# A gated mix of two attentions: gate, table and beta moved into the projections, a third buffer of q, and one output piece per run at the end

## Chip, cores and metric

The kernel runs on one core of a Trainium2 chip. The metric is the device time of one execution in microseconds (us). Before the change it is 1905.45 us, the median of three runs (1904.41 to 1909.33).

## What is computed

The reference, cut to what matters (S = 2048, D = 512, 32 heads of 16):

```
g = sigmoid((x * gate_w).sum(-1))            # one gate per row
a = softmax(q k' / 4) v @ A_wo               # side A: full attention, all rows
b = side B: per segment of 512 rows, causal softmax attention, mixed with a memory:
      o = sigmoid(beta) * a_mem + (1 - sigmoid(beta)) * a_dot      # one beta per head
      a_mem = phi(q) M / (phi(q) z);  then M += phi(k)' v, z += sum phi(k)
      b = o @ B_wo
out = g * a + (1 - g) * b
```

phi(t) is t + 1 for t > 0 and exp(t) otherwise.

## The kernel before

**Two stages.** The first, the projections, makes q, k and v of both sides and the memory's parts, and leaves them in DRAM tiles. The second, the attention, reads them back. The order of the instructions is written out by hand, for each engine, with no scheduler.

**The projections run in slots.** A slot (`slot`) is the 12 matmuls of one projection tile of 128 x 512: four steps of the contraction, three products each, since every operand is split into a rounded part and a rest. After each third matmul there is a place where posted work is issued: `post(slots, place, f)` counts from now, `post_at(n, place, f)` names the slot. Slots 0 to 47 are side A (for each of four chunks of 512 rows: four tiles of q, four of k, four of v), 48 to 95 are side B (q, v, k). `qk_tile` is a q or k tile: in the slot behind its matmuls ScalarE copies the PSUM tile out (`full`, L370) and casts it (`q1`, L371), VectorE takes the rest (`q2`, L378), and SP's queue stores both to DRAM (L372, L379). PSUM has two such tiles (`pr`), so a tile must be copied out before the second slot after its own begins. `q1` and `q2` have two buffers each. On side B, a tile with `then` also gets phi: a minimum on GpSimd (L375, tile `mn`), an exponential on ScalarE (L382), a sum on VectorE.

**Gate and beta.** `load_gate` (L456) brings 512 rows of x and, four and five slots later, `gate_logit` makes their logits on VectorE (L453). When all slots are through, the logits are transposed on TensorE, ScalarE makes the sigmoid (L572), VectorE one minus it, and GpSimd's queue stores both (L575); the attention's first exponential (L661) follows on ScalarE. Beta is brought spread over the partitions by eight loads on GpSimd's queue (L446, L449), and its sigmoids are made when side A's projections are through (L478, L479). ScalarE has its functions in tables, and the profile shows a load (ACT_TABLE_LOAD) where it goes from sigmoid to exponential or back.

**The attention runs in slots too.** There are 2368, 64 for each of 32 units of A (four heads, one chunk of queries) and 10 for each of 32 units of B. A slot makes one score tile (`st`, L638, three PSUM banks) and its exponential (L661). Side by side with it, 96 slots ahead (`LEAD`), runs a product for the row maxima (`sm`, L204, four banks) with its reduction on VectorE (L219). After each third slot (`BURST`) comes a run of P @ V (`some_values`, L694), and then at most one or two pieces of the output projection. A unit's sums go to DRAM (L699); `octet` brings eight heads back with their denominators, scales them with the gate, and `piece` (L771) multiplies them with the output weights, four matmuls of 32 columns in the program (the profile counts eight instructions).

**The end.** In the last 96 slots there are no maxima any more, so the four banks `sm` collect the last chunk's output (`close`): 80 pieces for five of its six octets of heads, in the list `fill`. After each run the loop takes one piece of it, or two where no maxima are left. The sixth octet (A's last) is known only after the last values: its sums go through DRAM, then come its 16 pieces, and after each four of them an addition into a tile `res` (two buffers) and the store of 128 rows (L881, L882).

Of the kernel before, what the change touches and what calls it, by code (L numbers as in the profile page):

```python
# [10 lines left out]
F32 = mybir.dt.float32  # L11
F32R = mybir.dt.float32r
AF = mybir.ActivationFunctionType
ALU = mybir.AluOpType
# [5 lines left out]
D = 512  # L20
H = 32
DH = 16
CH = 512
NCH = S // CH
KT = D // 128
NG = 8
NO = 4
# [20 lines left out]
def gated_mix(ctx, tc, x, xT, wqkv, a_wo, b_wq, b_wk, b_wv, b_wo, beta, gate_w, out):  # L48
    nc = tc.nc
# [14 lines left out]
    gd = dr.tile([2, S], F32, name="gd")  # L64
# [9 lines left out]
    identf = const.tile([128, 128], F32, name="identf")  # L74
# [32 lines left out]
    nS = len(slots)  # L107
# [22 lines left out]
    def raw(t):  # L130

        return t[:].bitcast(F32)
# [145 lines left out]
    with ExitStack() as p0:  # L278
# [12 lines left out]
        idle = me_ps.tile([128, CH], F32, tag="me", name="idle")  # L291
        for _ in range(10):
            nc.tensor.matmul(idle[:, :128], identf, identf, start=True, stop=True)
        ones = wk1.tile([2, CH], F32, name="ones")
        nc.vector.memset(ones, 1.0)
        for t in kbuf["A"] + kbuf["B"]:
            for r in range(2):
# [7 lines left out]
        def post(slots, place, f):  # L305
            posted.setdefault((now[0] + slots, place), []).append(f)
# [13 lines left out]
        def post_at(n, place, f):  # L320
            posted.setdefault((n, place), []).append(f)
# [35 lines left out]
        def xchunk(c):  # L357
            return xT[:, c * CH:(c + 1) * CH]

        def qk_tile(side, w, xc, o, dst, then=None):  # L360

            ps = pr_ps.tile([128, CH], F32, tag="pr", name="pr")
            slot(ps, lambda a, k: w[a][:, k, o * 128:(o + 1) * 128], lambda b, k: xc[b][:, k, :])
            full = wk.tile([128, CH], F32, tag="full", name="full")
            q1 = wk.tile([128, CH], F32R, tag="q1", name="q1")
            q2 = wk.tile([128, CH], F32R, tag="q2", name="q2")
            ph = {}

            def e0():
                nc.scalar.copy(full, ps)  # L370
                nc.scalar.copy(q1, full)  # L371
                nc.sync.dma_start(dst[0:16].rearrange("d h t -> (d h) t"), raw(q1))  # L372
                if then:
                    ph["mn"] = wk1.tile([128, CH], F32, tag="mn", name="mn")
                    nc.gpsimd.tensor_scalar_min(ph["mn"], full, 0.0)  # L375

            def e1():
                nc.vector.tensor_sub(q2, full, q1.bitcast(F32))  # L378
                nc.sync.dma_start(dst[16:32].rearrange("d h t -> (d h) t"), raw(q2))  # L379
                if then:  # L380
                    ph["ex"] = wk1.tile([128, CH], F32, tag="ex", name="ex")
                    nc.scalar.activation(ph["ex"], ph["mn"], AF.Exp)  # L382

# [57 lines left out]
        wAv = halves(wp, "wv", wqkv[:, 2 * D:3 * D], 1, 4, [pairs[1], None])  # L441
        gw = wk1.tile([128, D], F32, tag="gw", name="gw")
        nc.gpsimd.dma_start(gw, gate_w.unsqueeze(0).broadcast_to([128, D]))
        bt = wk1.tile([128, NO], F32, tag="bt", name="bt")
        for o in range(NO):
            nc.gpsimd.dma_start(bt[:, o:o + 1], beta[o * 8:(o + 1) * 8].unsqueeze(0).unsqueeze(2).broadcast_to([DH, 8, 1]))  # L446
        bt4 = wk1.tile([128, NO], F32, tag="bt4", name="bt4")
        for o in range(NO):
            nc.gpsimd.dma_start(bt4[:, o:o + 1], beta[o * 8:(o + 1) * 8].unsqueeze(1).unsqueeze(2).broadcast_to([8, 16, 1]))  # L449

        def gate_logit(xg, b, col):
            jk = wk1.tile([128, D], F32, tag="mn", name="jk")
# [3 lines left out]
        def load_gate(c):  # L456
            xg = []
            for i in range(2):
                xg.append(raws.tile([128, 2, D], F32, tag="raw", name="xg"))
                t0 = c * CH + 256 * i  # L460
                nc.sync.dma_start(xg[i], x[t0:t0 + 256, :].rearrange("(b p) d -> p b d", p=128))
            for b in range(4):
                post(4 + b // 2, 1 + 2 * (b % 2), lambda b=b: gate_logit(xg[b // 2], b % 2, 4 * c + b))

        for c in range(NCH):
# [9 lines left out]
                qk_tile("A", wAk, xc, o, kd["A", o, c])  # L475
            v_tiles("A", wAv, xc, c)
            xc = xn
        nc.scalar.activation(gh, bt, AF.Sigmoid)  # L478
        nc.scalar.activation(ogh, bt4, AF.Sigmoid)  # L479
        nc.vector.tensor_scalar(ogh, ogh, -1.0, 1.0, op0=ALU.mult, op1=ALU.add)  # L480

        mrun = [st.tile([128, 8, 17], F32, name=f"mrun{o}") for o in range(NO)]
        mbd = [st.tile([128, DH, 8], F32, name=f"mbd{o}") for o in range(NO)]
# [27 lines left out]
        def mem_k(o, c, pk, vs):  # L511
            tps = me_ps.tile([128, 4, 128], F32, tag="me", name="tps")
            for b in range(4):
                nc.tensor.transpose(tps[:, b], pk[:, b * 128:(b + 1) * 128], identf)
            pt = wk.tile([128, 4, 128], F32, tag="pt", name="pt", bufs=1)
            nc.scalar.copy(pt, tps)
            post(0, 3, lambda: mem_k2(o, c, pt, vs))

# [33 lines left out]
        for n in range(14, 64):  # L552
            if n // 12 > 2 or n % 12 < 8:
                post_at(s0 + n, 3, some_max)
        for c in range(NCH):
            for o in range(NO):
                then = (lambda pq, o=o, c=c: post(1, 1, lambda: mem_q(o, c, pq))) if c else None
                qk_tile("B", wBq, xc, o, qd["B", o, c], then)
            if c + 1 < NCH:
                xn = halves(xp, "x", xchunk(c + 1), now[0], now[0] + 3)  # L560
            post(2, 3, lambda c=c: load_gate(c))
# [7 lines left out]
        gps = me_ps.tile([128, CH], F32, tag="me", name="gps")  # L569
        nc.tensor.transpose(gps[:16, :128], glog, identf)  # L570
        gt = wk1.tile([128, 4, 128], F32, tag="ex", name="gt")
        nc.scalar.activation(gt[:16, 0], gps[:16, :128], AF.Sigmoid)  # L572
        nc.vector.tensor_scalar(gt[:16, 1], gt[:16, 0], -1.0, 1.0, op0=ALU.mult, op1=ALU.add)
        for i in range(2):
            nc.gpsimd.dma_start(gd[i].rearrange("(b t) -> b t", t=128), gt[:16, i])  # L575


    gp = ctx.enter_context(tc.tile_pool(name="gp", bufs=1, reuse_waits="tile"))
# [10 lines left out]
    fr = ctx.enter_context(tc.tile_pool(name="fr", bufs=1, reuse_waits="tile"))  # L589
# [188 lines left out]
    fill = []  # L778
# [63 lines left out]
    filled = [0]  # L842
    n = 0
    while n < nS or queue or beside or filled[0] < len(fill):
        for f in beside.pop(n, []):
            f()
        if n < nS:
            score_part(n)
        m = n + LEAD
        if m < nS:  # L850
            loads(m + PRE)

            def bank():
                i = free.pop(0)
                free.append(i)
                return banks[i]
            max_part(m, bank)
        run_todo(m)
        if n % BURST == BURST - 1 or n >= nS:
            if shared:  # L860
                for _ in range(4):
                    shared.pop(0)()
            else:
                some_values(n, MOST + jam(n) if n < nS else 8)

            if any(e[0] < m + 1 for e in late):
                run_late(st_ps, "st", m + 1)
            else:
                for _ in range(1 if m < nS else 2):
                    if filled[0] < len(fill) and fill[filled[0]][0] <= n:  # L870
                        fill[filled[0]][1]()
                        filled[0] += 1
        n += 1
    octet("A", NO - 1, last, None, vector=True)
    assert len(stored) == len(units)
    for b in range(4):
        for j in range(4):
            close(0, "A", NO - 1, b, j)
            fill.pop()[1]()
        t = fr.tile([128, D], F32, tag="res", name="res", bufs=2)  # L880
        nc.vector.tensor_add(t, banks[b], part[b])  # L881
        (nc.scalar if b % 2 else nc.sync).dma_start(out_rows(last, b), t)  # L882

# [34 lines left out]
```

## Time and profile before

| | before |
|---|---|
| median of three runs | 1905.45 us |
| time of the profiled execution | 1908.66 us |
| its span | 1906.9 us |
| mean granted TensorE clock | 0.989 |
| busy: TensorE, VectorE, ScalarE, GpSimd | 98%, 84%, 79%, 17% |
| DMA, mean over the span | 119 GB/s |

PE is TensorE's matmuls and PEld its weight loads, DVE is VectorE, ACT is ScalarE, POOL is GpSimd, SP is SyncE; a q behind a name is the engine's sequencer. L371 is line 371 of the kernel. A tile is written as out<-in. In a row of a group stand the count after x, then the busy time, the mean time of one in ns, and the idle time of the engine before these instructions with what ended it. In a timeline row stand the start, the length in us, and in brackets the idle time before and what ended it. PEclk is the clock that TensorE was granted, in tenths of full speed.

### The profile page before, as it was taken

The page shows a single profiled execution, that of the slowest core. Times are in us where ns is not written, and L with a number is a line of the kernel's source. Part 1 is how long each engine was busy: PE and PEld are TensorE (multiplying, and loading weights), DVE is VectorE, ACT ScalarE, POOL GpSimd, SP SyncE. Part 2 cuts the span into 40 slices and gives each one's busy share as a digit, 9 for nine tenths or more (in the row PEclk, how much of TensorE's full clock was granted, in tenths as well). Part 3 has the DMA queues.
Part 4 walks back from the last instruction along what each step waited for, and adds up shares of the span by engine and source line. Part 5 has one row for each costly group of instructions (what it writes and reads, how often), then busy time and mean ns, then how long its engine had stood idle before and what let it go on. Part 6 is the DMA issues. An engine that isn't in the chain of part 4 may idle for free.

```text
span 1906.9 us, 46497 instructions
## 1 busy us (share of the span) xinstructions
PE 1875.4 (98%) x18133; PEld 1014.6 (53%) x18133; DVE 1597.1 (84%) x2744; ACT 1508.1 (79%) x2928; POOL 319.1 (17%) x521
## 2 busy tenths in 40 slices
PE   8999999999999999999999999999999999999997
PEld 6887776455555554444444444444444454554554
DVE  4234677799999999999999999999999999999810
ACT  4445443798888898888888888888888888888874
POOL 3001221211111111121212111112121211111210
PEclk9999999799999999999999999999999999999998
DMA  6667645334233423343444343434333434343211
GB/s 207 206 226 243 205 169 183 114 99 131 87 108 94 109 86 109 100 112 100 112 100 112 100 107 104 111 97 115 98 107 105 108 100 113 101 112 101 77 56 44
DMA packets 124394, 227.32 MB, mean 119 GB/s; under 512 B 35176, under 2 KB 50184, under 8 KB 123664
## 3 DMA queue, kind: packets, MB, share of 16 engines
q1 hardware_dynamic: 122592, 223.24, 40.6%
q8 instruction: 144, 2.36, 0.5%
q0 software_dynamic: 1296, 0.59, 0.3%
q14 instruction: 74, 0.61, 0.1%
q10 hardware_dynamic: 288, 0.52, 0.1%
HBM read 155.52 MB, written 67.52 MB: 117 GB/s over the span
## 4 chain that ended last, share of the span: by engine, by line
PE 92%; ACT 3%; DMA 2%; DVE 1%; issue 1%; POOL 1%; SPq 0%; ACTq 0%; POOLq 0%; DVEq 0%
PE ops L694 31%; PE st L638 28%; PE sm L204 14%; PE pr L315 11%; PE ops L771 6%; ACT p L661 1%; PE sm L771 1%; DMA qdA<-q 1%; POOL mn L375 1%; PE mt_ps L194 1%; PE num L491 1%; ACT dg L230 0%; DMA vs<-wqkv 0%; DMA qdB<-q 0%; PE mps L522 0%
## 5 line engine op out<-in xcount | busy, mean ns | idle before, releaser
L661 ACT ACTIVATE p<-st 128x512 f32<-128x512 f32 x2304 | 1222.2, 604 | 185.7 <-PE sm L204 144.9
L219 DVE TENSOR_REDUCE pm<-sm 128x1 f32<-128x512 f32 x2048 | 1282.6, 683 | 75.7 <-PE sm L204 59.4
L204 PE MATMUL sm<-kA,qA 48*128 48x512 f32 x2048 | 742.9, 447 | 0.0
L638 PE MATMUL st<-qA,kA 50*128 50x512 f32 x2048 | 696.2, 439 | 6.6 <-ACT p L661 6.2
L694 PE MATMUL ops<-p,vA 128*17 128x512 f32 (+3 forms) x5848 | 560.3, 472 | 0.0
L638 PEld LDWEIGHTS st<-qA,kA 50*128 50x128 f32 x2048 | 334.4, 186 | 422.7 <-ACT p L661 355.9
L204 PEld LDWEIGHTS sm<-kA,qA 48*128 48x128 f32 x2048 | 334.1, 185 | 20.8 <-issue 6.5
L694 PEld LDWEIGHTS ops<-p,vA 128*17 128x17 f32 x5848 | 110.1, 96 | 176.9 <-issue 155.8
L204 PE MATMUL sm<-kB,qB 48*128 48x128 f32 (+2 forms) x896 | 170.8, 294 | 0.0
L204 PEld LDWEIGHTS sm<-kB,qB 48*128 48x128 f32 x896 | 137.4, 190 | 8.7 <-DVE pm L219 2.0
L231 POOL TENSOR_SCALAR_AFFINE_SELECT dg<-dg 128x512 f32<-128x512 f32 x128 | 81.5, 639 | 286.0 <-ACT dg L230 286.0
L378 DVE TENSOR_TENSOR q<-full,q 128x512 fp32r<-128x512 f32 x64 | 44.1, 689 | 97.8 <-ACT q L371 87.2
L187 POOL CAST ms<-nm 128x16 fp32r<-128x16 f32 x64 | 12.7, 198 | 650.6 <-DVE nm L180 416.2
L638 PE MATMUL st<-qB,kB 50*128 50x384 f32 (+3 forms) x512 | 119.1, 341 | 0.6 <-ACT mt L196 0.2
L638 PEld LDWEIGHTS st<-qB,kB 50*128 50x128 f32 x512 | 71.4, 185 | 65.7 <-ACT p L661 50.3
L642 POOL TENSOR_SCALAR_AFFINE_SELECT p<-p 128x512 f32<-128x512 f32 x128 | 79.1, 638 | 92.7 <-ACT p L661 90.5
L240 DVE TENSOR_REDUCE pmB<-sm 128x4 f32<-128x512 f32 x128 | 87.3, 682 | 0.5 <-PE sm L204 0.5
L234 DVE TENSOR_REDUCE pmB<-dg 128x4 f32<-128x512 f32 x128 | 86.8, 678 | 0.9 <-POOL dg L231 0.9
L694 PE MATMUL ops<-p,vB 128*17 128x128 f32 (+3 forms) x1192 | 86.5, 398 | 0.1
L370 ACT COPY full<-pr 128x512 f32<-128x512 f32 x64 | 37.3, 584 | 54.2 <-PE pr L315 54.1
L230 ACT COPY dg<-sm 128x512 f32<-128x512 f32 x128 | 76.3, 596 | 2.1 <-DVE pmB L234 2.1
L745 DVE RECIPROCAL rec<-rec 128x32 f32<-128x32 f32 x44 | 15.1, 344 | 70.9 <-DMA rec<-odA 36.7
(139 smaller groups left out, 1624.6 us busy)
## 6 DMA issues: line engine op xcount, KB each, us to landing
kA<-kdA SPq DMA_DIRECT2D x256, 128.0 KB
vA<-vdA SPq DMA_DIRECT2D x32, 544.0 KB
kA<-kdA SPq DMA_DIRECT2D x256, 64.0 KB
qdA<-q SPq DMA_DIRECT2D x32, 256.0 KB
kdA<-q SPq DMA_DIRECT2D x32, 256.0 KB
qdB<-q SPq DMA_DIRECT2D x32, 256.0 KB
qA<-qdA SPq DMA_DIRECT2D x64, 128.0 KB
kdB<-q SPq DMA_DIRECT2D x32, 256.0 KB
```

Source lines behind the costliest of these rows:

```text
L204: nc.tensor.matmul(ps[:, n0:n0 + n], rows(qt[u][:, :, s * 128:(s + 1) * 128], h, 48), rows(k[:, :, k0:k0 + n], h, 48), start=True, stop=True)
L219: nc.vector.tensor_reduce(pm[:, h, s, kc:kc + 1], ps, axis=AX.X, op=ALU.max)
L230: nc.scalar.copy(dg, blocked(ps))
L231: nc.gpsimd.affine_select(out=dg, in_=dg, pattern=[[0, 4], [-1, 128]], base=0, channel_multiplier=1, compare_op=ALU.is_ge, fill=MASKED)
L234: todo.append((m + MASK_T, lambda: nc.vector.tensor_reduce(to, dg.rearrange("p (h s) t -> p h s t", h=2), axis=AX.X, op=ALU.max)))
L240: nc.vector.tensor_reduce(pm[:, 1, h, 3:7], blocked(ps), axis=AX.X, op=ALU.max)
L315: nc.tensor.matmul(ps, l(a, k), r(b, k), start=(n == 0), stop=(n == 11))
L638: nc.tensor.matmul(ps[:, n0:n0 + CH - q0], rows(k[:, :, b * 128:(b + 1) * 128], h, 50), rows(q[:, :, q0:], h, 50), start=True, stop=True)
L642: nc.gpsimd.affine_select(out=x, in_=x, pattern=[[0, 4], [1, 128]], base=0, channel_multiplier=-1, compare_op=ALU.is_ge, fill=0.0)
L661: nc.scalar.activation(p[:, h], ps, AF.Exp, scale=SCALE)
L694: nc.tensor.matmul(ops[32 * h:32 * h + 17, q0:q0 + 128 * w], v[:, 17 * h:17 * h + 17], p[:, h, c0:c0 + 128 * w], start=(i == 0), stop=done ...
L771: nc.tensor.matmul(ps[32 * t:32 * t + 32, 128 * (j % (ps.shape[1] // 128)):128 * (j % (ps.shape[1] // 128)) + 128], held[side, c][:, o, 12 ...
```

## The change

Seven edits:

1. `ones` takes the buffer of `dn`; `pt` that of `am`.
2. `q1` and `q2` have three buffers.
3. Beta is loaded once as 8 x 4 and spread over the partitions by two products with spread-out identities (`betas`), with both sigmoids behind them, in slot 20. The eight loads and the sigmoids behind side A are gone.
4. The transpose and sigmoid of the gate and its two stores are a function `gates`, posted for slot 92 of 96; for this the last chunk's gate rows are loaded when the chunk begins (slot 84), six slots earlier than before.
5. Behind the sigmoid, `gates` makes one exponential of one element.
6. In the last slots one piece of `fill` follows a run of P @ V, not two; this holds behind the last slot too.
7. The last four results alternate between the buffers of `res` and `vM`.

```
-            q1 = wk.tile([128, CH], F32R, tag="q1", name="q1")
-            q2 = wk.tile([128, CH], F32R, tag="q2", name="q2")
+            q1 = wk.tile([128, CH], F32R, tag="q1", name="q1", bufs=3)
+            q2 = wk.tile([128, CH], F32R, tag="q2", name="q2", bufs=3)
...
-        for o in range(NO):
-            nc.gpsimd.dma_start(bt[:, o:o + 1], beta[o * 8:(o + 1) * 8].unsqueeze(0).unsqueeze(2).broadcast_to([DH, 8, 1]))
...
+        nc.gpsimd.dma_start(beta8, beta.rearrange("(o h) -> h o", h=8))
+        def betas():
+            ps = me_ps.tile([128, CH], F32, tag="me", name="bt")
+            spread = wk1.tile([8, 2, 128], F32, name="spread")
+            one8 = identf[0:8, 0:8]
+            nc.vector.tensor_copy(spread[:, 0].rearrange("p (d h) -> p d h", h=8), one8.unsqueeze(1).broadcast_to([8, DH, 8]))
+            nc.vector.tensor_copy(spread[:, 1].rearrange("p (h q) -> p h q", q=16), one8.unsqueeze(2).broadcast_to([8, 8, 16]))
+            for i, to in enumerate((gh, ogh)):
+                nc.tensor.matmul(ps[:, NO * i:NO * i + NO], spread[:, i], beta8, start=True, stop=True)
+                nc.scalar.activation(to, ps[:, NO * i:NO * i + NO], AF.Sigmoid)
+            nc.vector.tensor_scalar(ogh, ogh, -1.0, 1.0, op0=ALU.mult, op1=ALU.add)
+        post_at(20, 2, betas)
...
-        nc.scalar.activation(gh, bt, AF.Sigmoid)
-        nc.scalar.activation(ogh, bt4, AF.Sigmoid)
...
+        def gates():
+            gps = me_ps.tile([128, CH], F32, tag="me", name="gps")
+            nc.tensor.transpose(gps[:16, :128], glog, identf)
+            gt = wk1.tile([128, 4, 128], F32, tag="ex", name="gt")
+            nc.scalar.activation(gt[:16, 0], gps[:16, :128], AF.Sigmoid)
+            nc.scalar.activation(gt[:1, 2, 0:1], eps[:1], AF.Exp)
...
         for c in range(NCH):
+            if c + 1 == NCH:
+                load_gate(c)
+                post(8, 2, gates)
...
-                for _ in range(1 if m < nS else 2):
-                    if filled[0] < len(fill) and fill[filled[0]][0] <= n:
-                        fill[filled[0]][1]()
-                        filled[0] += 1
+                if filled[0] < len(fill) and fill[filled[0]][0] <= n:
+                    fill[filled[0]][1]()
+                    filled[0] += 1
...
-        t = fr.tile([128, D], F32, tag="res", name="res", bufs=2)
+        t = fr.tile([128, D], F32, tag="vM" if b % 2 else "res", name="res", bufs=2)
```

More of the change, by code (lines that the diff above doesn't have):

```diff
@@ L293, in gated_mix @@
             nc.tensor.matmul(idle[:, :128], identf, identf, start=True, stop=True)
-        ones = wk1.tile([2, CH], F32, name="ones")
+        ones = wk1.tile([128, CH], F32, tag="dn", name="ones")[0:2]
         nc.vector.memset(ones, 1.0)
@@ L443, in gated_mix @@
         nc.gpsimd.dma_start(gw, gate_w.unsqueeze(0).broadcast_to([128, D]))
-        bt = wk1.tile([128, NO], F32, tag="bt", name="bt")
-        for o in range(NO):
-            nc.gpsimd.dma_start(bt[:, o:o + 1], beta[o * 8:(o + 1) * 8].unsqueeze(0).unsqueeze(2).broadcast_to([DH, 8, 1]))
-        bt4 = wk1.tile([128, NO], F32, tag="bt4", name="bt4")
-        for o in range(NO):
-            nc.gpsimd.dma_start(bt4[:, o:o + 1], beta[o * 8:(o + 1) * 8].unsqueeze(1).unsqueeze(2).broadcast_to([8, 16, 1]))
+        beta8 = wk1.tile([8, NO], F32, name="beta8")
+        nc.gpsimd.dma_start(beta8, beta.rearrange("(o h) -> h o", h=8))
[10 more added lines that the diff above has]
+        post_at(20, 2, betas)
         def gate_logit(xg, b, col):
@@ L477, in gated_mix @@
             xc = xn
-        nc.scalar.activation(gh, bt, AF.Sigmoid)
-        nc.scalar.activation(ogh, bt4, AF.Sigmoid)
-        nc.vector.tensor_scalar(ogh, ogh, -1.0, 1.0, op0=ALU.mult, op1=ALU.add)
         mrun = [st.tile([128, 8, 17], F32, name=f"mrun{o}") for o in range(NO)]
@@ L514, in mem_k @@
                 nc.tensor.transpose(tps[:, b], pk[:, b * 128:(b + 1) * 128], identf)
-            pt = wk.tile([128, 4, 128], F32, tag="pt", name="pt", bufs=1)
+            pt = wk.tile([128, CH], F32, tag="am", name="pt", bufs=1).rearrange("p (b t) -> p b t", t=128)
             nc.scalar.copy(pt, tps)
@@ L554, in gated_mix @@
                 post_at(s0 + n, 3, some_max)
+        def gates():
[4 more added lines that the diff above has]
+            nc.scalar.activation(gt[:1, 2, 0:1], eps[:1], AF.Exp)
+            nc.vector.tensor_scalar(gt[:16, 1], gt[:16, 0], -1.0, 1.0, op0=ALU.mult, op1=ALU.add)
+            for i in range(2):
+                nc.gpsimd.dma_start(gd[i].rearrange("(b t) -> b t", t=128), gt[:16, i])
         for c in range(NCH):
+            if c + 1 == NCH:
+                load_gate(c)
+                post(8, 2, gates)
             for o in range(NO):
@@ L560, in gated_mix @@
                 xn = halves(xp, "x", xchunk(c + 1), now[0], now[0] + 3)
-            post(2, 3, lambda c=c: load_gate(c))
+            if c + 1 < NCH:
+                post(2, 3, lambda c=c: load_gate(c))
             vs = v_tiles("B", wBv, xc, c)
@@ L568, in gated_mix @@
             slot()
[L569 to L575, printed above, removed]
     gp = ctx.enter_context(tc.tile_pool(name="gp", bufs=1, reuse_waits="tile"))
```

## The prediction

> **What bounds the kernel now.** I read the page first, its clock row and its chain, then the waits of the projection stage, the table by stretches, the chain in order of time where the projections hand over to the attention, and the timeline of the end.
>
> ```profile
> PEclk9999999799999999999999999999999999999998
> PE 92%; ACT 3%; DMA 2%; DVE 1%; issue 1%; POOL 1%; SPq 0%; ACTq 0%; POOLq 0%; DVEq 0%
> ```
>
> TensorE carries 92% of the chain, and its clock is full but for one slice after the projections and the last one. So a gain has to come from places where TensorE stands still or runs slowly, or from work that is taken off it where it sets the pace. I find four such places, and the diff touches each.
>
> The first two are in the projections. The answers below are the waits of 0 to 36 us, then those of 142 to 180 us (total, times, longest), one line of the timeline, two pieces of the chain, one issue line and the stretches around both places (span, busy us of PE, PEld, DVE, ACT, POOL, granted clock, DMA share, GB/s).
>
> ```profile
> ACT q L371 <- DMA qdA<-q: 9.0, 3, 4.4
> PEld pr L315 <- ACT full L370: 5.0, 4, 2.9
> PE pr L315 <- ACT full L370: 3.5, 2, 2.5
> ...
> ACT q L371 <- DMA qdB<-q: 4.8, 1, 4.8
> PEld pr L315 <- ACT full L370: 2.6, 1, 2.6
> PE pr L315 <- ACT full L370: 2.2, 1, 2.2
> ...
> 26.98 0.62 ACT L371 CAST q<-full 128x512 fp32r<-128x512 f32 x1 [1.36 <-DMA qdA<-q]
> ...
> 24.12 8.81 DMA qdA<-q
> 151.23 7.21 DMA qdB<-q
> ...
> bt<-beta POOLq DMA_DIRECT2D x8, 0.5 KB, 8.3
> ...
> 24.00:28.00 4.00, 2.97 (x13) 2.13 (x12) 1.90 (x3) 2.64 (x6) 2.21 (x5) 1.00 0.20 64
> 32.00:36.00 4.00, 1.83 (x6) 1.46 (x7) 1.21 (x2) 1.72 (x3) 0.00 (x0) 0.85 0.94 342
> 36.00:40.00 4.00, 4.00 (x14) 3.19 (x13) 1.10 (x3) 2.02 (x4) 0.00 (x0) 0.73 0.90 344
> ...
> 157.60:161.00 3.40, 1.23 (x6) 0.73 (x5) 1.80 (x3) 2.44 (x5) 0.33 (x1) 1.00 0.92 348
> 160.00:164.00 4.00, 3.28 (x8) 2.61 (x9) 2.39 (x4) 2.29 (x5) 0.00 (x0) 0.63 0.73 267
> 164.00:168.00 4.00, 4.00 (x18) 3.25 (x17) 0.13 (x1) 1.21 (x2) 0.00 (x0) 0.94 0.98 299
> ```
>
> ScalarE's cast into q1 has two buffers, and waits until the store of the tile two slots earlier has landed. A landing takes 7 to 9 us there, while a slot of 12 matmuls lasts under 3. Behind the cast in ScalarE's order stands the copy that empties the next PSUM tile, and TensorE waits for that copy. The standstill then costs a second time: the clock drops to half.
>
> The third place is the handover (chain in order of time; start, length).
>
> ```profile
> 335.32 0.62 ACT q L371
> ...
> 335.96 1.28 ACT L572
> ...
> 337.25 0.27 ACT gt L572
> ...
> 337.54 1.28 ACT L661
> ...
> 338.83 0.61 ACT p L661
> ...
> 335.20:338.60 3.40, 1.24 (x10) 0.93 (x9) 1.63 (x4) 3.32 (x5) 0.79 (x2) 0.99 0.73 251
> 338.60:342.00 3.40, 2.52 (x11) 1.91 (x13) 2.18 (x4) 3.39 (x8) 0.36 (x1) 0.50 1.01 300
> 359.10:362.50 3.40, 3.40 (x31) 1.80 (x33) 2.19 (x4) 1.88 (x5) 0.00 (x0) 0.51 0.03 5
> ...
> L661 ACT ACTIVATE p<-st 128x512 f32<-128x512 f32 x27 | 14.3, 614 | 6.8 <-PE sm L204 6.8
> ...
> L661 ACT ACTIVATE p<-st 128x512 f32<-128x512 f32 x36 | 19.0, 606 | 2.2 <-PE sm L204 1.7 <-PE st L638 0.2
> ```
>
> ScalarE loads the sigmoid's table (L572), makes the gate, and loads the exponentials' table (L661) before the first exponential. The three score banks are full by then, TensorE stands, and its clock is at half until 362 us. The two group rows are exponentials from 338.7 to 362.9 us (27) and from 363.5 to 385.9 us (36).
>
> The fourth place is the end (timeline; the two counted rows are those of tile sm from 1819 to 1883.7 us, where a matmul is 272 ns).
>
> ```profile
> L771 PE MATMUL sm<-woB,vB x256: 272/273/273, 1819.5 to 1872.3; 128*32 128x128 f32 x128
> L771 PE MATMUL sm<-woA,vA x238: 272/273/273, 1841.0 to 1883.7; 128*32 128x128 f32 x119
> ...
> 1854.65 1.57 ACT L661 ACTIVATE p<-st 128x512 f32<-128x512 f32 x3 [0.51 <-PE st L638]
> ...
> 1872.46 0.73 PE L638 MATMUL st<-qA,kA 50*128 50x512 f32 x3
> ...
> 1884.93 0.59 ACT L698 COPY oraw<-ops 128x512 f32<-128x512 f32 x1 [1.53 <-PE ops L694]
> 1885.09 3.68 PE L771 MATMUL sm<-woB,vB 128*32 128x128 f32 x128
> 1896.58 6.25 PE L771 MATMUL sm<-woA,vA 128*32 128x128 f32 x128 [7.81 <-DVE vA L757]
> 1903.24 0.69 DVE L881 TENSOR_TENSOR res<-sm,part 128x512 f32<-128x512 f32 x1 [0.55 <-DMA out<-res]
> ```
>
> Until 1885 TensorE sets the pace: ScalarE waits 0.5 us for it in each run of three slots. Then TensorE waits 7.8 us for the trip of the last octet through DRAM, and its last 128 matmuls take 6.25 us where 128 like them took 3.68: half clock again.
>
> **The change part by part.**
>
> *Three buffers of q, and beta.* With three buffers the cast of slot 5 needs the store of slot 2, not of slot 3. In the first place the store of slot 2 had landed by 26.98 us, when the cast that waited for it began; slot 5's cast is due near 25 us, so it comes at most a slot late, and the copy behind it has a slot to spare. In the second, the fourth tile of the chunk is the first that has to wait at all, and the copies behind it have a slot to spare too. The eight beta loads took 8.3 us each to land for half a KB, in just the stretch where the stores were slow and the engines moved 64 GB/s; one load of 128 bytes replaces them. So I take both standstills as gone. Their size: at the first, between the 3.5 us of PE and the 5.0 us of PEld, so 4.3; at the second between 2.2 and 2.6, so 2.4. The clock lost with them is (1 - 0.85) x 4 + (1 - 0.73) x 4 = 1.7 us and (1 - 0.63) x 4 + (1 - 0.94) x 4 = 1.7 us. Together **10.1 us**. What is late next is nothing that the rows show: TensorE is busy without a break in the slots that follow. If the stores are as late as before and the third buffer only moves the wait, as little as 0 to 4 us of it comes.
>
> *Beta's product at slot 20.* TensorE gets two tiny matmuls behind two small VectorE copies, which have to be made in the same slot.
>
> ```profile
> 2.45 0.23 DVE L83 COPY bmask<-bsel 128x128 f32<-128x128 f32 x1
> 1827.43 0.38 PE L194 MATMUL mt_ps<-identf,ms 128*32 128x128 f32 x2
> ```
>
> The nearest rows: two copies of 0.23 us, if TensorE waits for both, and two pairs like the transposes of 0.38 us, 1.2 us in all; the lower end is 0, as both may pass beside the projections. I take **0.5 us** lost, nearer the copies, because VectorE has little else there. The sigmoid's table load and two short sigmoids move from the end of the A projections to this slot, on a ScalarE that is half idle in both.
>
> *The gate at slot 92.* Its transpose, sigmoid and one dummy exponential now follow the last gate logit by three slots. Their x loads go to SP at the start of the last chunk, six slots earlier, ahead of that chunk's stores and of nothing that is urgent; VectorE's four logits move from the last two slots to slots 88 and 89. On ScalarE two loads of 1.28 us and under 0.5 us of functions stand ahead of the copy that empties slot 92's PSUM tile.
>
> ```profile
> 321.70:325.30 3.60, 3.60 (x19) 2.45 (x17) 2.46 (x5) 0.57 (x2) 0.00 (x0) 1.00 0.85 245
> 325.30:328.90 3.60, 3.60 (x18) 2.47 (x16) 3.06 (x6) 1.19 (x3) 0.00 (x0) 1.00 0.99 410
> ```
>
> ScalarE is busy 0.57 and 1.19 us of these 3.6 us slots, and the tile is needed only one slot later, so about 3 us fit: cost 0. [...]
>
> What it saves: the first exponential can start when the last q cast ends, 335.94, not at 338.83: **2.9 us**. What is late next is ScalarE itself, whose next exponentials run one after another, and vA's load, which is issued after the last store as before. The gate's loads also leave GpSimd's queue before the diagonal masks need it.
>
> *The half clock after it.* The 27 exponentials from 338.83 to 363.57 took 24.7 us. The next 36 took 22.4 us at full clock, 0.622 a slot, so 27 would take 16.8: **7.9 us**, if the clock stays up. The case that it doesn't is a rival below.
>
> *One piece per run of P @ V.* A piece is 8 matmuls, and 16 pieces took 3.68 us, 0.23 each. By the rows 494 matmuls (of 496, two are past the edge), or 62 pieces, run before the last values; at one per run it is 31. So the last values come 31 x 0.23 = **7.1 us** earlier, as long as TensorE still sets the pace: a run of 1.57 + 0.51 = 2.08 us shrinks to 1.85, above ScalarE's 1.57. The 80 - 31 = 49 pieces left take 49 x 0.23 = 11.3 us after the last values, and the octet's trip takes 11.65 us (1884.93 to 1896.58) on other engines. They fill the wait and don't outlast it.
>
> *The last 16 pieces.* With at most half a us of standstill the clock should stay full. From 1896.58 to the end at 1906.9 is 10.3 us. At full clock: 3.7 us of matmuls, 0.15 us to the last add (an estimate), 0.69 us of add, and 2.97 us from its end to the span's end (1906.9 - 1903.93), in sum 7.5. The four result buffers remove the wait for an out store, which would grow once the matmuls are faster. **2.8 us**.
>
> Shared tiles (ones with dn, pt with am) cost nothing: the uses are several slots apart.
>
> Sum: 10.1 - 0.5 + 2.9 + 7.9 + 7.1 + 2.8 = 30.3 us. The profiled execution took 1908.66 us (span 1906.9 and 1.8 around it), which gives 1878.4. That execution is 3.2 us above the median of 1905.45; from the median it would be 1875.2. I say **1877**.
>
> **Rivals.**
>
> *The clock halves at the handover all the same.* In the first slots TensorE is paced by ScalarE, which needs 0.52 us an exponential (1.57 for three) and a copy beside some, while TensorE has a score and a maximum product to each; three of a kind take at most 0.73 us, and there are no values yet. As an estimate that is 60 to 85% busy in a stretch of 3.4 us. In the rows a stretch with 1.23 or 1.24 us of 3.4 (36%) lost the clock, and one with 2.97 of 4 (74%) kept it; these products use 48 or 50 rows of the array, so they may count for less. Then the 7.9 us don't come: 1885. [...]
>
> *The stores only wait elsewhere.* If the queue of transfers, not the number of buffers, sets the landing, 6 us of the 10.1 stay: 1883. For it: 342 to 348 GB/s in both places. Against it: the beta loads leave, and a third buffer gives a slot of 2.7 us at the second place, more than the 2.4 missing.
>
> *The end gives half.* Runs of P @ V paced by ScalarE after all, or the octet's trip longer with stores beside it: about 5 us less, 1882.
>
> *Slower: the half clock comes and stays.* After the handover it took 24 us to come back. At half clock 27 slots took 24.7 us for 16.8, a loss of 32%. Without the handover's 7.9 us the change gains 22.4; it turns into a loss once the half clock lasts 70 us longer than now, and at 100 us longer the time is 1917. Against it: 1500 us at full clock with such products.
>
> *It doesn't do what it says:* some function between the dummy exponential and the first real one loads another table, and the 1.28 us return. The cast at 335.32 ran without a load of its own, so I count this with the first rival.
>
> **How the numbers follow.** Forecast as worked out, 0.62; clock lost at the handover 0.16; stores 0.10; end 0.07; slower 0.03; the rest, 0.02, is no change. The forecast's own spread is some 5 us either way, from the two baselines and the bounds of the standstills. The range from 1868 to 1889 takes in the first three rivals with their spread. About 0.3%, 6 us, is what a measurement can tell here: faster 0.95, same 0.02, slower 0.03.
>
> **What would show it.** Right: no wait of PE for the copy in the first 36 us and at 150 us, clock 1.00 there; a first exponential less than 0.1 us after the last cast, no table load after slot 92; clock 1.00 from there to the end; some 390 matmuls of closing pieces (49 x 8) after the last values, and less than 1 us of wait before the last 128. Wrong: a clock row below 1 after the handover, or TensorE waiting for the last octet for several us again, or for ScalarE in slots 93 to 95.

## The result and the profile after

| | before | after |
|---|---|---|
| median | 1907.08 us (5 runs, 1904.41 to 1909.33) | 1892.9 us (5 runs, 1888.78 to 1898.7) |
| ratio, 95% interval | | 0.9932 [0.9907, 0.9956] |
| profiled execution, its span | 1908.66, 1906.9 us | 1898.7, 1896.7 us |
| its mean granted clock | 0.989 | 0.992 |

The change saves 14 us, not 28, and 1892.9 lies above the range. The profiled execution after is the longest of its five; with mean clocks of 0.992 to 0.997, the five spread over 10 us, and that spread is part of the answer.

From the page of after, the clock row and the chain:

```profile
PEclk9999999799999999999999999999999999999999
PE 92%; ACT 2%; DMA 2%; DVE 1%; issue 1%; POOL 1%; SPq 0%; ACTq 0%; POOLq 0%; DVEq 0%
```

The dip after the projections is still there. The table follows after's lead over before from event to event of the two profiled executions (each event is taken at its start, the last values at the start of their last group of matmuls). The last column is what the prediction had for the stretch.

| event | lead of after, us | gained in the stretch | predicted |
|---|---|---|---|
| slot 95 of the projections | 7.5 | 7.5 | 9.6 (10.1 - 0.5) |
| first exponential | 10.5 | 3.0 | 2.9 |
| 28th exponential | 8.7 | -1.8 | 7.9 |
| 2261st exponential | 8.9 | 0.2 | 0 |
| last values | 14.3 | 5.4 | 7.1 |
| end of the span | 10.2 | -4.1 | 2.8 |

Two rows are wrong in sign, the 28th exponential and the end; they account for 16.6 of the 20.1 us that are missing between 30.3 and 10.2.

**Projections.** The table by stretches of after, at both old standstills (span, busy us of PE, PEld, DVE, ACT, POOL, granted clock, DMA share, GB/s):

```profile
24.00:28.00 4.00, 4.00 (x19) 3.30 (x19) 2.18 (x4) 2.45 (x5) 0.00 (x0) 1.00 0.99 333
36.00:40.00 4.00, 4.00 (x20) 3.30 (x19) 0.00 (x0) 1.18 (x2) 0.00 (x0) 1.00 0.01 2
157.60:161.00 3.40, 3.40 (x16) 2.81 (x15) 0.00 (x0) 0.12 (x1) 0.00 (x0) 1.00 0.99 265
```

Before, PE was busy 2.97 of 4.00 us in the first of these, and 1.23 of 3.40 us in the third. Now it is busy throughout, the clock no longer falls, and TensorE no longer waits for the copy L370 in the first 36 us. A new loss is at slot 20, in after's timeline:

```profile
64.50 1.28 ACT L456 ACT_TABLE_LOAD   x1
65.39 0.38 PE L455 MATMUL bt<-beta,spread 8*128 8x4 f32 x2
65.81 0.17 ACT L456 ACTIVATE gh<-bt 128x4 f32<-128x4 f32 x1
66.03 0.38 PE L455 MATMUL bt<-beta,spread 8*128 8x4 f32 x2 [0.26 <-ACT gh L456]
```

The two products write one PSUM tile, `bt`, and a sigmoid reads it between them. So the second product waits for the first sigmoid (0.26 us idle, ended by `gh`), and that for its table load of 1.28 us: the slot took 4.10 us instead of 2.72.

**Handover.** After's timeline:

```profile
327.83 0.62 ACT L371 CAST q<-full 128x512 fp32r<-128x512 f32 x1
328.35 1.57 ACT L675 ACTIVATE p<-st 128x512 f32<-128x512 f32 x3
```

Its stretches from the last slots of the projections on, the columns as above:

```profile
324.90:328.70 3.80, 3.78 (x20) 2.54 (x18) 0.91 (x2) 2.26 (x5) 0.61 (x2) 1.00 0.65 221
328.70:332.10 3.40, 2.73 (x14) 1.62 (x14) 3.29 (x7) 3.40 (x8) 0.64 (x1) 1.00 0.81 273
332.10:335.50 3.40, 2.65 (x16) 1.17 (x15) 1.22 (x2) 2.21 (x5) 1.27 (x2) 0.50 0.99 257
352.60:356.00 3.40, 3.40 (x29) 1.79 (x31) 2.30 (x5) 1.99 (x5) 0.00 (x0) 0.50 0.00 0
356.00:359.40 3.40, 3.40 (x39) 1.36 (x35) 3.10 (x6) 2.68 (x6) 0.00 (x0) 1.00 0.28 84
```

The exponential follows the cast at once, no table load stands between them, and PE is busy 3.78 of 3.80 us up to there. Yet the granted clock is 0.50 from 332.1 on, after a stretch in which PE was busy 80%, and comes back only at 356.0. That is 23.9 us at half clock, as long as before the change (338.6 to 362.4).

**End.** After's timeline, from the last values on:

```profile
1870.69 0.59 ACT L712 COPY oraw<-ops 128x512 f32<-128x512 f32 x1 [1.12 <-PE ops L708]
1871.31 0.33 SPq L713 DMA_DIRECT2D odA<-oraw  x1
1874.10 3.76 PE L785 MATMUL sm<-woA,vA 128*32 128x128 f32 x128
1875.35 0.61 SPq L749 DMA_DIRECT2D rec<-odA  x1
1877.61 3.98 PE L785 MATMUL sm<-woB,vB 128*32 128x128 f32 x128
1879.71 0.32 SPq L764 DMA_DIRECT2D rdA<-rec  x1
1882.38 0.52 SPq L768 DMA_DIRECT2D inv<-rdA  x1
1886.55 6.33 PE L785 MATMUL sm<-woA,vA 128*32 128x128 f32 x128 [4.96 <-DVE vA L771]
```

The fills go on to 1881.6 (1877.61 + 3.98), 11 us behind the last values, as predicted. But the octet's trip, from the copy into `oraw` to the first of the last 128 matmuls, grew from 11.65 to 15.86 us. TensorE waits 4.96 us, and its last 128 matmuls take 6.33 us, the clock at 0.50 from 1885.2 to 1892.0 us.

### The profile page after: what moved, and what is told of

Its sections match the earlier page's. It is cut to its first block, busy times and chain, and to the rows that moved or that the text cites. A ratio compares the mean times of both kernels' runs of the same rounds, so it can differ in the third digit from the quotient of the medians.

```text
span 1896.7 us, 46501 instructions
## 1 busy us (share of the span) xinstructions
PE 1873.7 (99%) x18137; PEld 1013.2 (53%) x18137; DVE 1596.6 (84%) x2746; ACT 1508.4 (80%) x2929; POOL 315.0 (17%) x514
## 3 DMA queue, kind: packets, MB, share of 16 engines
q8 instruction: 144, 2.36, 0.5%
## 4 chain that ended last, share of the span: by engine, by line
PE 92%; ACT 2%; DMA 2%; DVE 1%; issue 1%; POOL 1%; SPq 0%; ACTq 0%; POOLq 0%; DVEq 0%
PE ops L708 31%; PE st L652 28%; PE sm L204 14%; PE pr L315 11%; PE ops L785 6%; ACT p L675 1%; PE sm L785 1%; POOL mn L375 1%; PE mt_ps L194 1%; PE num L497 1%; ACT dg L230 0%; DMA raw<-xT 0%; DMA qdB<-q 0%; DMA raw<-wqkv 0%; PE mps L528 0%
## 5 line engine op out<-in xcount | busy, mean ns | idle before, releaser
L370 ACT COPY full<-pr 128x512 f32<-128x512 f32 x64 | 37.4, 584 | 51.6 <-PE pr L315 51.4
```

## The experiments

Two theories for each of the three open losses. *The end*: either the trip is longer because instruction packets of 16 KB (queue 8; three in after's trip, one in before's) delay the small transfers, and TensorE's hundreds of short matmuls bring them (1), or it merely varies. *The clock*: either the granted clock goes with TensorE's busy time weighed by the rows of its products, 48 and 50 of 128 here (A), or with its busy time alone (A'). *The projections*: the standstills went by the third buffer, as predicted, or by the end of the eight beta loads (2).

**e1: the end as before.** The loop takes one piece where maxima are left and two after, as before; all else is as in the change.

```
-                if filled[0] < len(fill) and fill[filled[0]][0] <= n:
...
+                for _ in range(1 if m < nS else 2):
+                    if filled[0] < len(fill) and fill[filled[0]][0] <= n:
...
```

> The changed kernel with its sixth edit undone: two pieces follow a run of P @ V again. Measured from ScalarE's copy of the last sums to the first of the last 128 matmuls (the octet's trip through DRAM), the kernel before took 11.65 us with one packet of queue 8 (instructions, 16 KB) inside, and the changed kernel 15.9 us with three. Theory 1: the pieces that wait behind the last values make TensorE run through its instructions, and each 16 KB of instructions that is fetched holds up one of the 16 DMA engines for 1.3 to 1.7 us and with it a hop of the trip. It expects here 11.5 to 12.3 us with at most one packet, the last values 5 us later than in the changed kernel, and a time about 1 us over the changed kernel's (1893 to 1895, at the same share of half clock). Theory 2: the trip was slow by chance or by the transfers themselves; it expects 14 to 16 us here too and a time about 5 us over.

Measured: 1897.91 us (six runs, 1895.94 to 1900.61), ratio 0.9944 [0.9931, 0.9956]. The trip is 11.3 us with one instruction fetch in it, as (1) wants. The time is not: (1) expected 1893 to 1895 us. It is 5 us longer than the change's, or 2 to 4 us by the ratios to before (0.9944 against 0.9932, and 0.9922 in e8), and the last values end at 1877.42 and not at 1870.65. So the edit pays in a usual execution, less than the 7.1 us predicted for it.

**e2: fewer instructions at the end.** Behind the last slot, four pieces of 128 columns become one of 512, so that the closing matmuls are a quarter of the instructions.

```
+    def wide(side, o, b):
...
+        for t in range(4):
+            nc.tensor.matmul(banks[b][32 * t:32 * t + 32], held[side, last][:, o, 128 * b + 32 * t:128 * b + 32 * t + 32],
+                             wos[side][:, o], start=False, stop=(side, o) == closing[-1], tile_position=(0, 32 * t))
...
-                    fill[filled[0]][1]()
+                    if n >= nS and j == 0:
+                        wide(side, o, b)
+                        filled[0] += 4
...
```

> The changed kernel; but behind the last slot four pieces of 128 columns are one matmul of 512 columns for each of the four tiles of rows, the last 16 pieces as well. The same products in about the same TensorE time, with a quarter of the instructions. Theory 1 (instruction fetches hold up the trip): at most one packet of queue 8 during the trip, which takes 11.6 to 12.5 us in place of 15.9; TensorE then hardly waits, its clock stays full at the end, and from the copy of the last sums to the end it is 19 to 20 us in place of 26.0: 6 us faster than the changed kernel, near 1887. Theory 2 (TensorE at work, or chance, slows the transfers): the trip stays at 14 to 16 us and the time within 1.5 us of the changed kernel's 1892.9.

Measured: 1890.71 us (six runs, 1886.16 to 1894.36), ratio 0.9906 [0.9891, 0.9921]. Its timeline:

```profile
1870.24 0.59 ACT L712 COPY oraw<-ops 128x512 f32<-128x512 f32 x1 [1.12 <-PE ops L708]
1877.20 0.52 SPq L768 DMA_DIRECT2D inv<-rdA  x1
1881.51 3.64 PE L848 MATMUL sm<-woA,vA 128*32 128x512 f32 x32 [0.79 <-DVE vA L771]
```

The trip is 11.27 us, TensorE waits 0.79 us, and the clock holds for the last matmuls (1.00 from 1881 to 1885 us), as (1) wants. The median is only about 2 us below the change's, where (1) expected 6: the 15.86 us of after's trip are at the long end (12.3 to 15.63 us in e3, e4, e6, e7 and e8, whose ends are the same as the change's). The queue rows show the fetches. In after, for the 16 us of the trip (packets, MB, share of 16 engines):

```profile
q8 instruction: 3, 0.05, 1.5%
```

In before's trip, and on after's page for the whole execution:

```profile
q8 instruction: 1, 0.02, 0.4%
```

```profile
q8 instruction: 144, 2.36, 0.5%
```

A fetch is one packet of 16 KB (2.36 MB in 144 packets). In after three fall into the trip, one to each of its first three hops (at 1872.13, 1876.44 and 1880.25, taking 1.69, 1.25 and 1.03 us); before and in e2 it is one. They come with the count of TensorE's instructions: 381 matmuls and about as many weight loads were started in that trip, 132 in before's and 93 in e2's. The store of `oraw`, issued at 1871.31, shows how one delays it. It lands in 16 parts, 15 of them between 1873.12 and 1873.31 and the last at 1875.33; its last nine packets began only at 1873.81, when the fetch that had begun at 1872.13 was through (1873.82). In all six executions with three fetches this first hop took 3.07 to 4.04 us, in the four with one 2.01 to 2.39. The next two hops were longer in after (3.76 and 2.67 us) and e7 (3.37 and 3.20) alone, against 2.06 to 2.15 and 1.50 to 1.78 in the others: not every fetch in a trip delays it. TensorE's own matmuls run on beside the fetches here (128 in 3.76 us); what waited here were nine packets of the store, 1.68 us from the fetch's start (1872.13) to theirs (1873.81).

**e3 and e4: busy rows at the start.** After each of the first three runs of three slots TensorE makes one more product, of the identity with itself repeated to 512 columns, into the bank of P @ V, which is not yet in use; its clearing moves behind the first of them. In e3 the product has 128 rows, in e4 16; both take the same columns and instructions.

```
-    nc.vector.memset(ops, 0.0)
...
+        if n == 3:
+            nc.vector.memset(ops, 0.0)
...
+        if n % BURST == BURST - 1 and n < 9:
+            for _ in range(1):
+                nc.tensor.matmul(ops.rearrange("p (b t) -> p b t", t=128), identf[0:128], identf[0:128].unsqueeze(1).broadcast_to([128, 4, 128]),
+                                 start=True, stop=True)
```

> The changed kernel with one extra product of the identity (128 rows, 512 columns, 0.43 us at full clock) after each of the first three runs of the attention, into the bank of P @ V before its first values; the bank's clearing is issued three slots later for it. Theory A: the clock goes by the share of a stretch of 3.4 us in which TensorE streams, weighted with the rows in use; in the changed kernel that was 26% in the stretch before the clock fell (0.69 by time alone), and with the extra product it is near 50%. It expects full clock from 320 to 370 us in all or nearly all executions, mean clocks of 0.996 or more, and 6 to 8 us less than executions of the changed kernel that lost the clock there. Theory B: the clock falls because TensorE waits there at all; it expects the half clock of some 24 us as often as before and a time within 1 us.

> The same extra products, but of 16 rows of the identity: the same TensorE time (0.43 us each), an eighth of the rows. Theory A (weighted with rows): the stretch comes to about 29%, below what has kept the clock so far (44%), so the half clock after the handover comes as often as in the changed kernel (mean clock 0.992 to 0.994 in most executions). Theory A' (by time alone): over 0.9 of the stretch is busy, the clock stays full as with 128 rows, mean clocks of 0.996 or more.

Measured: e3 1887.18 us (four runs, 1886.26 to 1887.49), ratio 0.9889 [0.9876, 0.9902], mean clock 1.0 in all four. e4 1891.49 us (five runs, 1890.79 to 1894.37), ratio 0.9915 [0.9903, 0.9927], mean clock 0.994 to 0.997. The same stretches, of e3 and then of e4:

```profile
327.50:330.90 3.40, 3.38 (x19) 2.06 (x17) 2.46 (x5) 3.37 (x8) 0.57 (x1) 1.00 0.35 124
330.90:334.30 3.40, 3.21 (x14) 1.46 (x13) 2.33 (x4) 3.15 (x7) 0.70 (x2) 1.00 0.94 300
334.30:337.70 3.40, 1.72 (x17) 0.99 (x17) 0.32 (x1) 0.63 (x2) 0.64 (x1) 1.00 0.82 165
```

```profile
327.50:330.90 3.40, 3.38 (x18) 1.89 (x18) 1.97 (x4) 3.31 (x7) 0.08 (x1) 1.00 0.49 181
330.90:334.30 3.40, 3.40 (x11) 1.68 (x12) 1.54 (x3) 1.80 (x4) 1.19 (x2) 0.51 0.84 281
```

PE is busy 3.38 of 3.40 us in both, then e4's clock is halved and e3's is not, even after a stretch with 1.72 us busy. So busy time alone does not tell the two apart, and (A) stands: with 128 rows in the three products the clock held at 1.00, with 16 it went to 0.51.

The ten traces put a size to it. In each of them the clock changes on a grid of 3.41 us (in before, for example, it stays at one value for 3.41, 10.24, 23.89, 27.31 or 122.88 us: 1, 3, 7, 8 and 36 times 3.41). Count every matmul from its start to the next one's start, or to its end if that is earlier, and weigh it by its rows over 128. As an estimate, the windows of that grid at the handover are then:

| execution | window from | busy by time | weighed by rows | clock after it |
|---|---|---|---|---|
| before | 335.1 | 0.38 | 0.17 | half |
| after | 328.7 | 0.80 | 0.31 | half |
| e4 | 327.5 | 0.99 | 0.30 | half |
| e1, e8, e2 | 330.2, 329.9, 331.8 | 0.83, 0.82, 0.86 | 0.32, 0.31, 0.33 | half |
| e3, its lowest | 333.3 | 0.45 | 0.45 | full |
| e5, e6, e7, with extra products | 329.5, 332.3, 332.4 | 1.00, 0.99, 1.00 | 0.60, 0.60, 0.60 | full |

Over all of the ten executions, 20 of the 21 windows that lost the clock come to 0.41 at most by rows, and all of the some 5400 that kept it to 0.44 or more; the exception is one of 0.55 at 5.2 us in e5, which lost it. Weighed by the columns of the array as well, they don't sort: windows of 0.21 to 0.30 keep the clock all through the attention, and those of 0.30 to 0.33 above lost it. Products of 50 rows come to 50/128 = 0.39 even without a gap between them, so by this estimate a window with nothing but scores and maxima stands with those that lost the clock (0.41 or less), however busy TensorE is in it.

The clock is worth 4.3 us against e4 in the same set of runs, and 5.4 us against e8 (1892.57, another set); 6 to 8 were expected. With it, the 27 exponentials took 21.25 us, against 26.56 after and 16.8 in the forecast. One part of the rest is that the first values still wait for `vA` (e3's timeline):

```profile
335.98 0.84 PE L707 MATMUL ops<-p,vA 128*17 128x384 f32 x8 [1.86 <-DMA vA<-vdA]
```

In e6, e5 and e7, at full clock there too, this wait is 0.66, 0.25 and 0 us, and the 27 exponentials take 20.04, 19.62 and 19.32 us. Another part may be the extra products themselves, which keep TensorE 1.05 us each (the first in e3 from 328.48 to 329.53 us); the 0.43 expected was the author's figure, which no run shows. Nor does a run show the full clock there without them.

**e6 and e7: the two edits in the projections, one undone at a time.** Both start from e3, whose clock is steady. e6 takes the third buffers away:

```
-            q1 = wk.tile([128, CH], F32R, tag="q1", name="q1", bufs=3)
-            q2 = wk.tile([128, CH], F32R, tag="q2", name="q2", bufs=3)
+            q1 = wk.tile([128, CH], F32R, tag="q1", name="q1")
+            q2 = wk.tile([128, CH], F32R, tag="q2", name="q2")
```

> The changed kernel with the extra products of 128 rows (1887.2, full clock, so that little noise is left), and q1 and q2 with two buffers as before; beta is loaded once. Theory 1, the buffers remove both standstills: the slots 5 to 8 and 52 to 53 get long again, 5 to 9 us in all, 1892 to 1896. Theory 2, the eight small beta loads made the first standstill by holding up the stores: slots 5 to 8 stay within 1 us of 2.72 each, only 52 and 53 get long, 3 to 4 us, near 1890.5.

Measured: 1889.75 us (four runs, 1888.67 to 1890.76), ratio 0.9903 [0.989, 0.9916], 2.6 above e3. The second standstill is back and little of the first (slot 5 takes 3.23 us), in its waits of 0 to 36 us (total, times, longest):

```profile
PEld pr L315 <- ACT full L370: 0.9, 2, 0.8
...
PE pr L315 <- ACT full L370: 0.4, 1, 0.4
```

And of 142 to 180 us:

```profile
PEld pr L315 <- ACT full L370: 2.4, 1, 2.4
PE pr L315 <- ACT full L370: 2.0, 1, 2.0
```

e7 keeps three buffers and brings back the eight beta loads, with their sigmoids behind side A.

```
-        nc.gpsimd.dma_start(beta8, beta.rearrange("(o h) -> h o", h=8))
...
+        for o in range(NO):
+            nc.gpsimd.dma_start(bt[:, o:o + 1], beta[o * 8:(o + 1) * 8].unsqueeze(0).unsqueeze(2).broadcast_to([DH, 8, 1]))
...
+        for o in range(NO):
+            nc.gpsimd.dma_start(bt4[:, o:o + 1], beta[o * 8:(o + 1) * 8].unsqueeze(1).unsqueeze(2).broadcast_to([8, 16, 1]))
...
```

> The same base (1887.2) with three buffers of q, but beta comes by the eight loads as before and its sigmoids stand behind side A's projections; the products in slot 20 are gone. Theory 1 (buffers): slots 5 to 8 take 2.72 us each or nearly, slot 20 gets its 1.4 us back: 1885.5 to 1886.5. Theory 2 (beta loads): slots 5 to 8 lose 1 to 4 us in spite of the third buffer: 1887 to 1890.

Measured: 1894.81 us (four runs, 1890.71 to 1897.42), ratio 0.9926 [0.9908, 0.9943], 7.6 above e3. Its waits of 24 to 46 us:

```profile
ACT q L371 <- DMA qdA<-q: 5.7, 2, 4.3
PE pr L315 <- ACT full L370: 4.0, 1, 4.0
```

Its stretches there:

```profile
32.00:36.00 4.00, 0.82 (x4) 0.36 (x2) 1.09 (x2) 1.00 (x2) 0.00 (x0) 0.93 1.03 395
36.00:40.00 4.00, 3.23 (x8) 2.56 (x9) 3.15 (x5) 3.38 (x7) 0.00 (x0) 0.50 0.57 216
```

GpSimd's DMA queue from 20 to 36 us, in e7 and then in e3:

```profile
q0 software_dynamic: 385, 0.29, 18.4%
```

```profile
q0 software_dynamic: 165, 0.28, 4.5%
```

With three buffers the standstill is still there, one wait of 4.0 us, only now at slots 8 and 9 (6.83 and 5.29 us) and not at slots 5 to 8. For about the same bytes (0.29 and 0.28 MB) GpSimd's queue holds 18.4% of the engines in e7 and 4.5% in e3, which is 13.9% of 16 engines for 16 us, or 36 us of engine time for loads of half a KB. So (2) holds in the first place, and the third buffer is what removed the second. A short wait in the first place can still come with both remedies: in e2's execution slot 5 took 4.04 us. e7 lost more than the 1887 to 1890 us that (2) expected. In the traces its projections end 4.8 us behind e3's; 1.9 us of that come back in the first 27 exponentials, where `vA` is no longer waited for, and 2.8 us are left at the copy into `oraw`. Another 5.7 us come behind it, with a trip of 15.63 us against e3's 12.51 and half clock behind it, where no load of beta runs.

**e8: the change again**, unedited.

> The changed kernel once more, on the same chip as the others. If its spread of 10 us (1888.8 to 1898.7) comes from where the clock falls and how the instruction fetches meet the octet's trip, executions with a higher mean clock are the shorter ones, by about 0.95 us for each 0.0005 of mean clock (1890 us x 0.0005), with 2 to 4 us left for the trip; the median stays at 1891 to 1895.

Measured: 1892.57 us (six runs, 1889.66 to 1897.96), ratio 0.9922 [0.9907, 0.9937]. Its profiled execution took 1890.81 us, 7.9 less than after's. It had 13.65 us of half clock at the start of the attention and a trip of 13.1 us, where after's had 23.9 and 15.86. Its 27 exponentials took 22.87 us, 3.7 less than after's, and from the copy into `oraw` to the end it took 22.16 us, 3.8 less. So both causes vary from execution to execution, and in these two they make nearly all of the difference; for the other executions only their mean clocks are known.

**e5: the remedies together.** It has e3's extra products, e2's wide pieces, and both products of beta ahead of both sigmoids, two slots behind the copies:

```
+                for i in range(2):
+                    nc.tensor.matmul(ps[:, NO * i:NO * i + NO], spread[:, i], beta8, start=True, stop=True)
+                for i, to in enumerate((gh, ogh)):
+                    nc.scalar.activation(to, ps[:, NO * i:NO * i + NO], AF.Sigmoid)
...
+            post(2, 2, product)
```

> Three edits on the changed kernel together: the extra products of 128 rows in the first three runs, the pieces of 512 columns behind the last slot, and beta's two products ahead of both sigmoids, two slots after the copies that they need (in the changed kernel the second product waits behind the first sigmoid and its table load, and slot 20 takes 4.10 us in place of 2.72). If the causes are independent, it is the 1887.2 of the extra products, less 1.2 us for a trip of 11.3 in place of 12.5, less 1.2 at slot 20: 1884 to 1886, at a mean clock of 0.999 or 1. If the wide pieces or the product's place have a price of their own, it stays at 1887 or above.

Measured: 1883.87 us (four runs, 1883.33 to 1885.73), ratio 0.9874 [0.9862, 0.9887], mean clock 0.999 to 1.0, trip 11.1 us; 1884 to 1886 were expected if the causes add up. It beats both kernels: 24.6 us below before in the same set of runs (1908.47), and its times spread over 2.4 us, not 10. Slot 20 is back at 2.72 us, but slot 22, where the products now are, takes 3.47.

## Why the prediction was right or wrong

**The sign and the four places were right, the size was not.** Terms in the order of the sum:

- *Standstills, 10.1: right in size, half right in cause.* 9.1 us came. The third buffer is what the prediction's step rested on; e6 and e7 show that it carries the second place only. In the first, the beta loads did it, which the prediction named beside the buffer without choosing. What is late next is `vA`, whose load the prediction named at the handover without a price: waiting for it took back 1.2 and 1.9 us of what e3 gained over e6 and e7 in the projections. Its rival "the stores only wait elsewhere" is what e7 shows once the beta loads are back.
- *Beta at slot 20, 0.5: too small, 1.4.* The bound priced copies and products, and left out the wait of the second product for a sigmoid behind a table load, though it named the table load. One tile for two products with a reader between them made a chain of what was costed as parts.
- *Handover, 2.9: right*, 3.0. Both table loads of 1.28 us (316.59 and 318.17 us) stand in slot 92, and no wait of TensorE for ScalarE showed in slots 93 to 95.
- *Half clock, 7.9: wrong, -1.8.* The step that failed is that the clock stays up once the handover is short. The first rival, given 0.16, is what happened. The prediction even had its argument, that products of 48 and 50 rows may count for less, and set a stretch with 74% busy against it; that stretch was of 128 rows. The error was to compare busy shares across stages with different rows. The runs show in its place that the clock was lost after windows of at most 0.41 by rows (and one of 0.55), and after's window was 0.31 (0.80 by time). The lead even shrank; the first values now wait 0.75 us for `vA`, which may be a part of it. The term may have been too large in itself: at full clock the runs show 19.32 to 21.25 us, with the extra products in them, and none shows the 16.8. In e4 the clock was halved even after 3.38 us busy of 3.40.
- *Runs of P @ V, 7.1: 5.4.* The price of 0.23 us a piece held only where TensorE set the pace. Over the last runs the starts of exponentials three apart go from 2.08 to 1.90 us in the even part, and from 2.50, 2.07, 1.87, 1.51 to 2.33, 1.87, 1.71, 1.45 in the last: in the shortest run of four ScalarE is the limit (three exponentials 0.48 us apart), and in after's timeline nine exponentials stand nearly without a gap.

```profile
1852.58 4.72 ACT L675 ACTIVATE p<-st 128x512 f32<-128x512 f32 x9 [0.33 <-PE st L652]
1857.51 0.73 PE L652 MATMUL st<-qA,kA 50*128 50x512 f32 x3
1858.04 1.57 ACT L675 ACTIVATE p<-st 128x512 f32<-128x512 f32 x3 [0.74 <-PE st L652]
```

- *Last pieces, 2.8: wrong, -4.1.* The step that failed is "they fill the wait and don't outlast it": 49 pieces did take 11 us, but the trip was taken as given. The work that was to hide it made it longer, by its own instruction fetches (three packets of 16 KB in after's trip, one in before's); the third rival had only "stores beside it" for that. The 4.1 us are those of one execution: in e8's, the stretch from `oraw` to the end takes 22.16 us against 21.97 before, a loss of 0.2. In e5, where the cover costs few instructions, the stretch from `oraw` to the end takes 18.55 us, against 21.97 before: 3.4 us, more than the 2.8. The 0.15 us to the last add, an estimate, is 0.14 us in e2, e3 and e5.

With the three causes mended (e5), 24.6 of the 30.3 us are there.

**Left open.** Why the clock comes back after 13.65, 17.07 or 23.9 us in the attention (four, five and seven times 3.41 us), and after 3.41 or 6.83 us (e7) in the projections. By the estimate above, the first window of at least 0.69 by rows ends it in five of the six executions that lost it at the handover, and in them no window of less does; but in e1 it stayed through one of 0.67 and came back after one of 0.63. Open too is why a fetch delays the second and third hop in two executions and not in the others.

## To carry to other kernels

Before a gain is booked for "the clock stays up", look at how many rows of the array the matmuls of that stage use: here a TensorE busy 3.38 of 3.40 us with products of 16 to 50 rows went to half clock (e4), and three products of all 128 rows in the same places held it at 1.00 (e3, 4.3 us less). Where a kernel's executions spread, read more than one trace before a loss in one of them is taken for the usual one. Cover for a wait is not free when the wait is a chain of small transfers: 381 short matmuls went with three instruction fetches and a trip of 15.86 us (after), 93 wide ones with one and 11.27 us (e2). Two products that share a PSUM tile with a reader between them run in that reader's time: slot 20 took 4.10 us here and not 2.72.

## What the hardware did that was not expected

- Sixteen against 128 rows in three products moved the time by 4.3 us (1891.49 and 1887.18) and the mean clock from 0.994–0.997 to 1.0.
- Weighed by rows, a window of 3.41 us lost the clock at 0.41 or less and kept it at 0.44 or more, but for one in the start of e5 (0.55); by time alone, windows of 0.80 to 0.99 lost it.
- The half clock at the handover lasts a multiple of 3.41 us, four times (e8) and seven times (after) in executions of one and the same kernel.
- Three instruction fetches of 16 KB went with trips of 12.3 to 15.9 us (e6, e3, e4, e8, e7, after), one with 11.1 to 11.7 us (e5, e2, e1, before).
